# An adaLN block with linear attention and SwiGLU: scale weight in column halves, a fold in three groups, turned weight loads in halves

## The chip, the core and the metric

The kernel runs on one core of a Trainium2 chip. The metric is the device time of one execution in microseconds (us), the median of several runs. TensorE (PE) does matmuls, VectorE (DVE) and ScalarE (ACT) the element work, GpSimd (POOL) small element work and some DMA issues, SyncE (SP) most DMA issues.

## The reference

x is [1, 2048, 1024] in bf16, c is [1, 1024]. Cut to what matters:

```python
mod = (silu(c) @ w_mod).reshape(1, 6, 1, 1024)         # sa, ca, ga, sb, cb, gb
h = layernorm(x) * (1 + ca) + sa
q, k, v = heads(h @ wqkv)                              # 32 heads of 32
pq, pk = phi(q), phi(k)                                # phi(t) = elu(t) + 1 + 1e-6
kv, z = sum_s pk v, sum_s pk
o = (pq kv) / (pq z + 1e-6)
x = x + ga * (o @ wo)
h = layernorm(x) * (1 + cb) + sb
out = x + gb * ((silu(h @ w_gate) * (h @ w_up)) @ w_down)   # inner width 3584
```

## The kernel before, in words

The 2048 tokens are four blocks (sc) of 512, each of four tiles (t) of 128; D = 1024 is eight chunks (cc) of 128. For each block there is a K phase, a V phase and a Q phase of 64 matmuls each (128x128 stationary, 512 moving columns), a kv_phase (lines 335 to 348) that sums phi(K) V per head into kv_acc, and later den (the denominators), wo_tile (lines 631 to 660: attention output times wo, first residual, second layernorm), gate_up (448 matmuls) and down (224). All are issued to TensorE in the order in which the program text calls them: `mm` (line 97) keeps program order. Other engines are ordered by a scheduler, with hand-set anchors (`issue_after`) and, in the start, a fixed order (`in_order`, line 83). Loads are issued on the SP queue in order; where one must follow another, `last_load` (line 117) carries the anchor. Tiles come from pools: k8 (19 buffers of 8 KB per partition, all the big tiles, `big`, line 103) and two PSUM pools of four banks, pa (`acc_a`) and pb (`acc_b`).

**Start (lines 124 to 145 and 465 to 529).** V of block 0 comes first. The first block isn't modulated ahead of V: V uses hs = normalised x times (1 + ca), and the shift sa is added later through vb (line 595). The loads go out in the order x tile 0 and 1, eight chunks of the ca columns of w_mod (wca, tile name wme, 128x1024 each), then wv with x tiles 2 and 3 between, the sa columns (wsa), wk. c is turned on TensorE, passed through Silu (line 479) into scT, and the scale is made by row matvecs with w_mod (`mod_rows`, line 255: four matmuls of 256 columns per chunk into four column groups, and one one-column matmul for the first chunk), turned on DVE (line 263) and multiplied into hs (lines 498 to 504). xn is transposed on TensorE (line 217) and copied by DVE into hT. `keep_warm` matmuls on zeros (lines 456 to 463) fill the waits. sc_row, Silu(c) as a row in all partitions, is made by eight broadcast matmuls and two ACT copies (lines 485 to 489).

**The other blocks.** hT(sc+1) is made in block sc: layernorm (line 242), a transposing DMA per tile on the SP queue (line 239), then eight DVE multiply-adds over 128x512 (`modulate`, line 213, called at line 579). K of block sc+1 needs the result at once (line 543).

**Turned w_mod loads (lines 374 to 398).** The vectors ga, sb and cb are computed on DVE: `mod_load(q)` loads the columns of vector q transposed (two DMAs, each 512 columns, 1 MB, into wmt), and `mod_step` multiplies one 128x1024 piece with sc_row and sums it. The loads of vector 2 (ga) go out at the end of block 0 (line 588), those of 3 (sb) after three K groups of block 1 (line 547), those of 4 (cb) in block 3 (line 558). In block 2 the eight loads of wo go out at that place (lines 550 to 556). `hold_back` (line 369) writes one element of a tile on DVE, so that its load is not issued earlier.

**The fold (lines 602 to 627).** KV is folded into wo: for each half h of the heads, each column half nb and each g, four matmuls (i = 0 to 3) of 32x32 with 512 columns, stationary KVT rows of group g (row group g of the array) and output columns i (column group i). One call does (h, nb) with g = 0 to 3: 16 matmuls, all at different positions of the array, into four PSUM tiles "wf", copied back over wo. The calls stand between Q groups of blocks 1 and 2 (lines 618 to 627).

The lines that the prediction names: L98 is every matmul (helper `mm`), L101 every transpose on TensorE, L121 x loads, L214 modulate, L239 the transposing DMA of hT, L380 the turned load, L498 the first scale, L556 the wo loads.

Of the kernel before, what the change touches and what calls it, by code (L numbers as in the profile page):

```python
# [21 lines left out]
def kernel(  # L22
# [13 lines left out]
    nc = tc.nc  # L36
# [77 lines left out]
    c_sb = const.tile([DC, P], BF16, name="c_sb")  # L114

# [8 lines left out]
    for st in range(2):  # L124
        load_x(st, nc.sync)
# [3 lines left out]
    wca = [big("wme", [4, D]) for _ in range(2)]  # L129
# [6 lines left out]
    for j in range(DC):  # L136
        load_block(wca, wm_v, j, D, nc.scalar if j == 0 else nc.sync)
    for cc in range(DC):
        load_block(wv, wqkv_v, cc, 2 * D)
        if cc in (1, 4):  # L140
            load_x(2 + cc // 4, nc.sync)
# [26 lines left out]
    sc_row = const.tile([P, D], BF16, name="sc_row")  # L168
# [11 lines left out]
    sel = const.tile([P, HPC, P], BF16, name="sel")  # L180
# [17 lines left out]
    def bn(src, mv_out):  # L198
        stats = small.tile([P, NNB, nc.vector.BN_STATS_DIM], F32, name="stats")
        for i in range(NNB):  # L200
            nc.vector.bn_stats(out=stats[:, i, :], in_=src[:, i * NB:(i + 1) * NB])  # L201
        nc.vector.bn_aggr(out=mv_out, in_=stats[:])

    def normalise(dst, src, mean, rstd):
        nc.vector.tensor_scalar(out=dst, in0=src, scalar1=mean, scalar2=rstd, op0=ALU.subtract, op1=ALU.mult)

    def normalise_act(dst, src, mv, rstd):
        nmr = small.tile([P, 1], F32, name="nmr")
        last_nmr[0] = nc.gpsimd.tensor_scalar(out=nmr[:], in0=mv[:, 0, 0:1], scalar1=rstd[:, 0:1], scalar2=-1.0,  # L209
                                op0=ALU.mult, op1=ALU.mult)  # L210
        nc.scalar.activation(out=dst, in_=src, func=ACT.Identity, bias=nmr[:], scale=rstd[:, 0:1])  # L211
# [5 lines left out]
    def pe_transpose_tile(hT, xn, t):  # L217
        tp = acc_b("tp", (DC, P), BF16)
        for cc in range(DC):
            transpose(tp[:, cc, :], xn[:, cc * P:(cc + 1) * P])  # L220
        nc.vector.tensor_copy(out=hT[:, :, t * P:(t + 1) * P], in_=tp[:])
# [3 lines left out]
    def ln1_stats(sc, t):  # L225
        x_sb = x_tiles.pop(sc * STC + t)
        mv = small.tile([P, STC, 2], F32, name="mv")
        bn(x_sb, mv[:, 0, :])
        rstd = rstd_of(mv, 1)
        return sc, t, x_sb, mv, rstd  # L230

    def ln1_norm(sc, t, x_sb, mv, rstd, dve=False):
        xn = k2.tile([P, D], BF16, name="xn", bufs=4)
        if dve:
            normalise(xn[:], x_sb[:], mv[:, 0, 0:1], rstd[:, 0:1])
        else:
            normalise_act(xn[:], x_sb[:], mv, rstd)
        if sc > 0:
            last_load[0] = nc.sync.dma_start_transpose(hTs[sc][:, :, t * P:(t + 1) * P], xn[:])  # L239
        return xn  # L240
# [14 lines left out]
    def mod_rows(q, lo, hi, first=None):  # L255
        for j in range(lo, hi):
            if first is not None:
                mm(first, lhsT=wca[j // 4][:, j % 4, 0:P], rhs=scT[:, j:j + 1], start=False, stop=j == DC - 1)
            row_matvec(mod_ps[:, q * MW:(q + 1) * MW], sc32[:, j, :], (wsa, wca)[q][j // 4][:, j % 4, :],
                       q == 0 and j == 0, j == DC - 1)  # L260
# [4 lines left out]
    def scale_to(hs, hT, cc, lo, hi):  # L265
        nc.vector.tensor_scalar(out=hs[:, cc, lo:hi], in0=hT[:, cc, lo:hi], scalar1=ca0T[:, cc:cc + 1], scalar2=None,
                                op0=ALU.mult)

# [105 lines left out]
    def mod_load(q, cols, held=False):  # L374
        ts = [big("wmt", [DC // 2, D]) for _ in range(2)]
        if held:
            hold_back(ts)
        for h, t in enumerate(ts):
            lo = q * D + h * NB
            last = nc.sync.dma_start_transpose(t[:], w_mod[:, lo:lo + NB])  # L380
            mod_steps.extend((t[:, i, :], cols[:, 4 * h + i:4 * h + i + 1]) for i in range(DC // 2))
        return last
# [71 lines left out]
    nc.vector.memset(sel[:], 0.0)  # L454

    def keep_warm(acc, n):
        for _ in range(n):
            mm(acc[:], lhsT=sel[:, 0, :], rhs=sel[:], start=True, stop=True)

    def keep_warm_f32(acc, n):  # L460
        zeros = sel[:].rearrange("p h n -> p (h n)").bitcast(F32)
        for _ in range(n):
            mm(acc[:, 0:zeros.shape[1]], lhsT=zeros[:, 0:P], rhs=zeros, start=True, stop=True)

    accs = [acc_a() for _ in range(4)]
    spare = accs[3]
    keep_warm_f32(spare, 3)
    keep_warm(spare, 1)
# [5 lines left out]
    with in_order(nc.vector, nc.scalar, nc.gpsimd):  # L474
        mod_ps = acc_b("mod_ps")
        mm(mod_ps[:, 0:DC], lhsT=c_sb[:], rhs=ident[0:DC, 0:DC], start=True, stop=True)
        for g in range(4):
            mm(mod_ps[g * DH:(g + 1) * DH, MW:2 * MW], lhsT=ident[:, 0:DH], rhs=base_t[:, 0:MW], start=True, stop=False)
        nc.scalar.activation(out=scT[:], in_=mod_ps[:, 0:DC], func=ACT.Silu)
        xn0 = ln1_norm(*ln1_stats(0, 0))  # L480
        st1 = ln1_stats(0, 1)
        nc.vector.tensor_copy(out=sc32[:], in_=scT[:].unsqueeze(2).to_broadcast([P, DC, DH]))
        xn1 = ln1_norm(*st1, dve=True)
        keep_warm_f32(spare, 1)
        for h in range(2):
            for j in range(DC // 2):
                mm(accs[h][:, j * P:(j + 1) * P], lhsT=scT[:, 4 * h + j:4 * h + j + 1].to_broadcast([P, P]), rhs=ident[:],
                   start=True, stop=True)
            nc.scalar.copy(out=sc_row[:, h * NB:(h + 1) * NB], in_=accs[h][:])
        keep_warm(spare, 3)  # L490
        first = accs[2][:, 0:1]
        mm(first, lhsT=ident[:], rhs=base_t[:, 0:1], start=True, stop=False)
        mod_rows(1, 0, 3, first)
        pe_transpose_tile(hT, xn0, 0)
        pe_transpose_tile(hT, xn1, 1)
        mod_rows(1, 3, DC, first)
        keep_warm(spare, 1)
        nc.vector.tensor_scalar(out=hs[:, 0, 0:H], in0=hT[:, 0, 0:H], scalar1=first, scalar2=None, op0=ALU.mult)  # L498
        mod_turn(DC, 2 * DC)
        for cc in range(1, 4):  # L500
            scale_to(hs, hT, cc, 0, H)
        xn2 = ln1_norm(*ln1_stats(0, 2))
        for cc in range(4, DC):
            scale_to(hs, hT, cc, 0, H)
        st3 = ln1_stats(0, 3)
        gs = k_groups[0:4]
        v_mms(hs, gs, accs, 0, 6)
        pe_transpose_tile(hT, xn2, 2)
        for cc in range(DC):
            scale_to(hs, hT, cc, H, H + P)  # L510
        xn3 = ln1_norm(*st3)
        v_mms(hs, gs, accs, 6, DC)
        gs2, accs2 = k_groups[4:6], [acc_b("acc") for _ in range(2)]
        v_mms(hs, gs2[0:1], accs2[0:1])
        v_evac(0, gs, accs)
        pe_transpose_tile(hT, xn3, 3)
        for cc in range(DC):
            scale_to(hs, hT, cc, H + P, SCW)
        v_mms(hs, gs2[1:2], accs2[1:2])
        mod_rows(0, 0, DC)  # L520
        mod_turn(0, DC)
        nc.vector.tensor_copy(out=sca[:], in_=scr[:, :, :, 0])
        v_evac(0, gs2, accs2)
        for g in k_groups[6:8]:
            acc = acc_a()
            v_mms(hs, [g], [acc])
            v_evac(0, [g], [acc])
        modulate_all(hT, ca1T, saT)
# [4 lines left out]
    for h in range(2):  # L533
        with tc.issue_after(last_load[0].ins):
            nc.sync.dma_start(out=wq[h][:], in_=wqkv_v[:, 4 * h:4 * h + 4, 0:D])
# [5 lines left out]
    for sc in range(NSC):  # L541
        if sc > 0:
            k_phase(sc, 0, 2)
            kv_phase(sc - 1)
            k_phase(sc, 2, 3)
            if sc == 1:
                mod_load(3, sbT, True)
                mod_step(1)
            k_phase(sc, 3, 4)
            if sc == 2:  # L550
                wo = [big("wo", [4, D]) for _ in range(2)]
                hold_back(wo)
                for h in range(2):
                    for g in range(4):
                        with tc.issue_after(last_load[0].ins):
                            last_load[0] = nc.sync.dma_start(out=wo[h][g * DH:(g + 1) * DH, :, :], in_=wo_v[h, g])  # L556
            if sc == 3:
                mod_load(4, cbT, True)
            k_phase(sc, 4, 8)
        if sc == 0:  # L560
            k_phase(0, 0, 8)
# [24 lines left out]
        if sc == 0:  # L586
            with tc.issue_after(last_load[0].ins):
                last_load[0] = mod_load(2, gaT)

    q_phase(1, 0, 1, 2)  # L590
    q_phase(1, 1, 2)
# [10 lines left out]
    def fold_wo(h, nb):  # L602
        ns = slice(nb * NB, (nb + 1) * NB)
        ps = [acc_b("wf") for _ in range(4)]
        for i in range(HPC):
            for g in range(4):
                rs = slice(g * DH, (g + 1) * DH)
                mm(ps[g][i * DH:(i + 1) * DH, :], lhsT=KVT[rs, h, i * DH:(i + 1) * DH], rhs=wo[h][rs, i, ns],
                   start=True, stop=True)
        for g in range(4):  # L610
            (nc.scalar.copy if g % 2 == 0 else nc.vector.tensor_copy)(out=wo[h][:, g, ns], in_=ps[g][:])

    q_phase(1, 2, 5)
# [5 lines left out]
    den_sum(0, acc_a())  # L619
    fold_wo(0, 0)  # L620
    den_spread(0)
    q_phase(1, 6, 8)
    fold_wo(0, 1)
    q_phase(2, 0, 2)
    fold_wo(1, 0)
    q_phase(2, 2, 4)
    fold_wo(1, 1)
# [3 lines left out]
    def wo_tile(st):  # L631
# [10 lines left out]
        for nb in range(NNB):  # L642
            ns = slice(nb * NB, (nb + 1) * NB)
            a_ps = acc_b("a_ps")
            for hg in range(HG):
                mm(a_ps[:], lhsT=pq[:, hg, t * P:(t + 1) * P], rhs=wo[hg // 4][:, hg % 4, ns],
# [145 lines left out]
```

## Time and profile before

| what | value |
|---|---|
| median of 9 runs | 829.86 us (829.49 to 830.24) |
| profiled execution | 829.49 us, of which span 827.7 us |
| PE busy | 823.3 us, 4609 matmuls |
| DVE, ACT, POOL busy | 348.8, 168.1, 63.9 us |
| first V matmul, first K matmul of block 0 | 10.98, 26.86 us |
| K of block 1, 2, 3 starts | 54.49, 83.37, 112.26 us |
| the four fold groups start | 154.40, 158.32, 162.25, 166.17 us |

The span is the time between the first and the last instruction of the profiled execution; 1.8 us of its own time lie around it. In the timelines each row is a run of like instructions: start in us, length in us, engine, line, operation, output and inputs by the program's names, shape, count, and in brackets the idle time ahead of it and what ended it. The granted clock of TensorE is 1.00 in every window.

### The profile page before, as it was taken

Reading aid. Unit: us, or ns where it says so; the run is one execution under the profiler, and the core shown is the slowest. Engines: PE = TensorE matmul, PEld = TensorE weight load, DVE = VectorE, ACT = ScalarE, POOL = GpSimd, SP = SyncE. Lnnn points to the kernel's source line nnn. Section 1 sums busy time; section 2 is a strip of 40 time slices with the busy share of each in tenths; the row PEclk is TensorE's granted clock in tenths of the full one; section 3 lists DMA queues with packets and bytes.
Section 4 is the critical chain, followed back from the end, with each engine's and each line's share of the span. In section 5 each row is a group of like instructions: output and inputs, shape, how many; then the busy total and the mean of one; then the engine's idle time right before and its main releaser. Section 6 shows DMA issues by size and latency. Waiting matters only on the chain.

```text
span 827.7 us, 11287 instructions
## 1 busy us (share of the span) xinstructions
PE 823.3 (99%) x4609; PEld 379.5 (46%) x4609; DVE 348.8 (42%) x680; ACT 168.1 (20%) x253; POOL 63.9 (8%) x165
## 2 busy tenths in 40 slices
PE   9999999999999999999999999999999999999998
PEld 5444444444444444444444444444444444444444
DVE  6879778886353344421111353211114432222222
ACT  3545443434111101101111010111111101111000
POOL 2101020120312001000000010000001100000000
PEclk9999999999999999999999999999999999999999
DMA  9978444239996836456252272753405529610011
GB/s 351 297 167 195 117 111 102 45 104 324 367 226 201 256 106 184 147 172 206 88 164 90 65 224 88 254 184 109 146 0 183 149 68 358 217 44 1 19 58 51
DMA packets 142212, 129.07 MB, mean 156 GB/s; under 512 B 58768, under 2 KB 120720, under 8 KB 141648
## 3 DMA queue, kind: packets, MB, share of 16 engines
q1 hardware_dynamic: 138208, 115.10, 46.2%
q0 software_dynamic: 3792, 12.98, 5.2%
q8 instruction: 36, 0.59, 0.3%
q10 hardware_dynamic: 160, 0.26, 0.1%
q14 instruction: 16, 0.13, 0.1%
HBM read 101.98 MB, written 12.72 MB: 139 GB/s over the span
## 4 chain that ended last, share of the span: by engine, by line
PE 99%; DVE 0%; issue 0%
PE acc L98 91%; PE a_ps L98 7%; PE kvp L98 1%; PE mod_ps L98 0%; PE tp L101 0%; PE wf L98 0%; PE den L98 0%; PE vb L98 0%; DVE e L708 0%; DVE ob L711 0%; DVE sel L454 0%; DVE neg_half L150 0%
## 5 line engine op out<-in xcount | busy, mean ns | idle before, releaser
L98 PE MATMUL acc<-h2T,wgu 128*128 128x512 bf16 x1792 | 387.6, 379 | 0.0
L98 PEld LDWEIGHTS <-wgu 128*128 128x128 bf16 x1792 | 175.2, 98 | 211.3
L687 DVE TENSOR_TENSOR gu<-acc,e 128x512 bf16<-128x512 f32 x112 | 77.5, 692 | 289.9 <-PE acc L98 289.9
L98 PE MATMUL acc<-wd,gu 128*128 128x512 bf16 (+2 forms) x924 | 196.1, 373 | 0.0
L686 ACT ACTIVATE e<-acc 128x512 f32<-128x512 f32 x112 | 66.9, 597 | 374.8 <-PE acc L98 374.8
L98 PEld LDWEIGHTS <-gu 128*128 128x128 bf16 x924 | 89.3, 98 | 104.4
L708 DVE TENSOR_TENSOR e<-acc,gb_bc 128x512 f32<-128x512 f32 (+2 forms) x33 | 22.3, 676 | 131.7 <-PE acc L98 128.8
L98 PEld LDWEIGHTS <-hT 128*128 128x128 bf16 x448 | 43.6, 98 | 52.2
L98 PE MATMUL a_ps<-wo,pq 128*128 128x512 bf16 x256 | 57.4, 379 | 0.0
L98 PE MATMUL acc<-hT,wq 128*128 128x512 bf16 x256 | 56.7, 379 | 0.0
L98 PE MATMUL acc<-wk,hT 128*128 128x512 bf16 x256 | 56.4, 379 | 0.0
L273 ACT ACTIVATE eb<-acc 128x512 bf16<-128x512 f32 x64 | 37.6, 594 | 61.3 <-PE acc L98 59.0
L211 ACT ACTIVATE xn<-x,nmr,rstd 128x1024 bf16<-128x1024 f32 x16 | 19.8, 1240 | 126.2 <-POOL nmr L209 126.2
L98 PE MATMUL acc<-wv,hT 128*128 128x512 bf16 x192 | 41.9, 379 | 0.0
L98 PEld LDWEIGHTS <-pq 128*128 128x128 bf16 x256 | 25.1, 98 | 30.2
L655 POOL DMA_DIRECT2D x_scratch<-x x16 | 9.8, 615 | 373.9 <-DVE x L648 373.8
L98 PEld LDWEIGHTS <-wq 128*128 128x128 bf16 x256 | 24.6, 98 | 29.9 <-issue 1.1
L274 DVE TENSOR_SCALAR eb<-eb 128x512 bf16<-128x512 bf16 x64 | 18.4, 291 | 25.6 <-ACT eb L273 25.4
L648 DVE TENSOR_TENSOR x<-a_ps,x_sb 128x512 f32<-128x512 f32 x32 | 22.1, 691 | 8.6 <-PE a_ps L98 8.6
L195 POOL TENSOR_TENSOR rstd<-veps,neg_half 128x1 f32<-128x1 f32 x32 | 17.9, 559 | 98.4 <-DVE veps L193 86.3
L201 DVE BATCH_NORM_STATS2 stats<-x_sb 128x6 f32<-128x512 bf16 x32 | 21.0, 675 | 4.5 <-DMA x_sb<-in_A_x_dram 4.4
L711 DVE TENSOR_TENSOR ob<-e,x1r 128x512 bf16<-128x512 f32 (+2 forms) x33 | 22.3, 675 | 1.0
(99 smaller groups left out, 322.2 us busy)
## 6 DMA issues: line engine op xcount, KB each, us to landing
wgu<-in_B_w_gate_dram SPq DMA_DIRECT2D x28, 1024.0 KB, 6.9
wgu<-in_B_w_up_dram SPq DMA_DIRECT2D x28, 1024.0 KB, 8.0
x_sb<-in_A_x_dram SPq DMA_DIRECT2D x32, 256.0 KB, 5.3
x_scratch<-x POOLq DMA_DIRECT2D x16, 512.0 KB, 3.1
x1r<-x_scratch SPq DMA_DIRECT2D x31, 256.0 KB, 2.9
wd<-in_B_w_down_dram SPq DMA_DIRECT2D x7, 1024.0 KB, 6.6
rbc<-rden_scratch POOLq DMA_DIRECT2D x16, 256.0 KB, 8.8
out_dram<-ob SPq DMA_DIRECT2D x31, 128.0 KB, 1.7
```

Source lines behind the costliest of these rows:

```text
L98: return tc.keep_in_program_order(nc.tensor.matmul(out, lhsT=lhsT, rhs=rhs, start=start, stop=stop))
L195: nc.gpsimd.tensor_tensor(out=rstd[:, 0:n], in0=veps[:, 0:n], in1=neg_half[:].to_broadcast([P, n]), op=ALU.pow)
L201: nc.vector.bn_stats(out=stats[:, i, :], in_=src[:, i * NB:(i + 1) * NB])
L211: nc.scalar.activation(out=dst, in_=src, func=ACT.Identity, bias=nmr[:], scale=rstd[:, 0:1])
L273: nc.scalar.activation(out=e[:], in_=acc, func=ACT.Exp)
L274: nc.vector.tensor_scalar(out=e[:], in0=e[:], scalar1=1.0, scalar2=PHI_EPS, op0=ALU.min, op1=ALU.add)
L648: nc.vector.tensor_tensor(out=x1[:, ns], in0=a_ps[:], in1=x_t[:, ns], op=ALU.add)
L655: nc.gpsimd.dma_start(out=x1_dram[st * P:(st + 1) * P, :], in_=x1[:])
L686: nc.scalar.activation(out=sg[:], in_=ps[0][:], func=ACT.Silu)
L687: gm = nc.vector.tensor_tensor(out=guT[sc][f // GPT][:, f % GPT, :], in0=ps[1][:], in1=sg[:], op=ALU.mult)
L708: nc.vector.tensor_tensor(out=yt, in0=y_ps, in1=gb_bc[:, ns], op=ALU.mult)
L711: nc.vector.tensor_tensor(out=ob, in0=yt, in1=x1r, op=ALU.add)
```

## The change

1. *Loads of the start.* Three x tiles first. wca is loaded in two halves of 512 columns, each as four DMAs of 128x2x512 (rows of 1 KB); wv chunks 0 to 3 stand between the halves, x tile 3 and wv 4 to 7 behind.
2. *sc_row.* The broadcast matmuls and ACT copies go. c is loaded as a row, Silu is taken of the row on ACT, it is written to DRAM by POOL and loaded back into all partitions on the SP queue behind wq.
3. *First block.* The scale of chunks 0 to 3 is made as columns by 32 one-column matmuls, that of chunks 4 to 7 by 32 row matmuls of 128 columns inside the V stage. V of the first four groups starts with chunk 0 and goes on as pieces come; hs is scaled directly from PSUM, hT is copied by ACT. All zero-matmuls are f32, of 512, 256 or 128 columns. K of block 0 does its first two groups interleaved.
4. *Turned loads.* (vector 2, half 0) at the end of block 0; (2, half 1) and (3, half 0) in block 1; (3, half 1) in block 2 ahead of the wo loads, which are anchored on it; both halves of 4 in block 3, as before. kv_phase moves from behind K group 1 to behind K group 0.
5. *Fold.* The 16 units (h, nb, g) of four matmuls are done in groups of 5, 6 and 5 units instead of 4 x 4, at three places instead of four, into new tiles wof that wo_tile reads. The PSUM tiles come from both pools.

```diff
-    for st in range(2):
+    for st in range(3):
         load_x(st, nc.sync)
...
-    wca = [big("wme", [4, D]) for _ in range(2)]
+    wca = [big("wme", [DC, NB]) for _ in range(2)]
...
+    def load_ca(h, eng0):
+        for k in range(4):
+            js = slice(2 * k, 2 * k + 2)
+            (eng0 if k == 0 else nc.sync).dma_start(out=wca[h][:, js, :], in_=wm_v[:, js, D + h * NB:D + (h + 1) * NB])
+
+    load_ca(0, nc.scalar)
+    nc.scalar.dma_start(out=sc_row[0:1, :], in_=c)
+    for cc in range(4):
         load_block(wv, wqkv_v, cc, 2 * D)
-        if cc in (1, 4):
-            load_x(2 + cc // 4, nc.sync)
+    load_ca(1, nc.sync)
+    load_x(3, nc.sync)
+    for cc in range(4, DC):
+        load_block(wv, wqkv_v, cc, 2 * D)
...
+        def ca_cols(k):
+            for i in range(4):
+                for j in (2 * k, 2 * k + 1):
+                    mm(cols[i], lhsT=wca[0][:, j, i * P:(i + 1) * P], rhs=scT[:, j:j + 1], start=False,
+                       stop=j == DC - 1 and i in (0, 3))
+
+        mm(cols[0], lhsT=ident[:], rhs=base_t[:, 0:1], start=True, stop=False)
+        mm(mod_ps[:, DC:DC + 3], lhsT=ident[:], rhs=base_t[:, 0:3], start=True, stop=False)
+        keep_warm(NB)
+        ca_cols(0)
+        keep_warm(NB, 2 * P)
+        ca_cols(1)
+        turn_half(xn0, 0, 0)
+        ca_cols(2)
+        keep_warm(P)
+        turn_half(xn0, 0, 1)
+        turn_half(xn1, 1, 0)
+        ca_cols(3)
+        keep_warm(P)
...
+        gs = k_groups[0:4]
+        v_mms(hs, gs, accs, 0, 1)
+        turn_half(xn1, 1, 1)
+        nc.scalar.copy(out=hT[:, 4:8, 0:H], in_=tps[1][:])
+        nc.scalar.activation(out=sc_row[0:1, :], in_=sc_row[0:1, :], func=ACT.Silu)
+        v_mms(hs, gs, accs, 1, 3)
+        tp2 = turn_tile(xn2)
+        for cc in range(4):
+            scale_turned(tp2, cc, 2)
+        nc.scalar.copy(out=hT[:, :, H:H + P], in_=tp2[:])
+        v_mms(hs, gs, accs, 3, 4)
+        ca_rows()
...
+    nc.gpsimd.dma_start(out=sc_dram[:], in_=sc_row[0:1, :])
+    with tc.issue_after(wq_load.ins):
+        nc.sync.dma_start(out=sc_row[:], in_=sc_dram[:].to_broadcast([P, D]))
...
         if sc > 0:
-            k_phase(sc, 0, 2)
+            k_phase(sc, 0, 1)
             kv_phase(sc - 1)
-            k_phase(sc, 2, 3)
+            k_phase(sc, 1, 3)
             if sc == 1:
-                mod_load(3, sbT, True)
+                mod_load(2, gaT, (1,), True)
+                mod_load(3, sbT, (0,), True)
                 mod_step(1)
             k_phase(sc, 3, 4)
             if sc == 2:
+                last_load[0] = mod_load(3, sbT, (1,), True)
                 wo = [big("wo", [4, D]) for _ in range(2)]
...
         if sc == 0:
             with tc.issue_after(last_load[0].ins):
-                last_load[0] = mod_load(2, gaT)
+                last_load[0] = mod_load(2, gaT, (0,))
...
+    wof = [big("wof", [4, D]) for _ in range(2)]
+    fold_units = [(h, nb, g) for h in range(2) for nb in range(NNB) for g in range(4)]
+
+    def fold_wo(accs):
+        units = [(fold_units.pop(0), acc) for acc in accs]
         for i in range(HPC):
-            for g in range(4):
+            for (h, nb, g), acc in units:
                 rs = slice(g * DH, (g + 1) * DH)
...
-    den_sum(0, acc_a())
-    fold_wo(0, 0)
+    den_sum(0)
+    fold_wo([acc_b("wf") for _ in range(3)] + [acc_a() for _ in range(2)])
     den_spread(0)
     q_phase(1, 6, 8)
-    fold_wo(0, 1)
-    q_phase(2, 0, 2)
-    fold_wo(1, 0)
-    q_phase(2, 2, 4)
-    fold_wo(1, 1)
+    q_phase(2, 0, 1)
+    fold_wo([acc_b("wf") for _ in range(4)] + [acc_a() for _ in range(2)])
+    q_phase(2, 1, 4)
+    fold_wo([acc_b("wf") for _ in range(4)] + [acc_a()])
```

## The prediction

> **What bounds the kernel now.** I read the page's busy line first, then its chain of waits, then the timeline of each engine around every place that the diff touches.
>
> ```profile
> PE 823.3 (99%) x4609; PEld 379.5 (46%) x4609; DVE 348.8 (42%) x680; ACT 168.1 (20%) x253; POOL 63.9 (8%) x165
> ...
> PE 99%; DVE 0%; issue 0%
> ```
>
> TensorE (PE) is busy 823.3 of 827.7 us, and the chain that ended last is TensorE too. So a transfer or a vector operation costs nothing until TensorE waits for it, and a change pays or costs only by (a) the length of the matmul stream, (b) a wait put into it, (c) the start ahead of it. There are three such places. The first is the start (timeline of TensorE from 0; columns: start us, length us, engine, operation, count):
>
> ```profile
> 7.18 0.17 PE L98 MATMUL acc<-eb,ident 128*128 128x1 bf16 x1
> 7.21 0.16 PE L98 MATMUL acc<-scT,wme 128*128 128x1 bf16 x1
> ...
> 10.98 5.35 PE L98 MATMUL acc<-wv,hs 128*128 128x512 bf16 x24
> ...
> 22.41 1.06 PE L98 MATMUL mod_ps<-wme,sc 128*32 128x256 bf16 x32
> 23.40 3.63 PE L98 MATMUL acc<-wv,hs 128*128 128x512 bf16 x16
> 26.86 5.34 PE L98 MATMUL acc<-wk,hT 128*128 128x512 bf16 x24
> ```
>
> The first V matmul starts at 10.98 and the first K matmul at 26.86. From there the stream has no gap until the end beyond about 0.09 us where the shape of matmuls changes. The second place is the fold of wo (timeline of TensorE from 153):
>
> ```profile
> 153.84 0.63 PE L98 MATMUL acc<-pq,Zden 128*32 128x128 bf16 x32
> 154.40 0.43 PE L98 MATMUL wf<-wo,kvs 32*32 32x512 bf16 x16
> 154.76 3.63 PE L98 MATMUL acc<-hT,wq 128*128 128x512 bf16 x16
> 158.32 0.43 PE L98 MATMUL wf<-wo,kvs 32*32 32x512 bf16 x16
> 158.69 3.63 PE L98 MATMUL acc<-hT,wq 128*128 128x512 bf16 x16
> ```
>
> Sixteen 32x32 matmuls of 512 columns take 0.367 us together (154.40 to 154.76): each has a tile position of its own, they start 3.3 ns apart, and 317 ns after the last start the next full matmul starts. The third place is the load of hT(3), the normalised block 3 (timelines of SyncE, VectorE and TensorE):
>
> ```profile
> 62.86 8.50 SPq L380 DMA_TRANSPOSE wmt<-in_w_mod_dram  x2
> ```
> ```profile
> 93.91 3.65 SPq L556 DMA_DIRECT2D wo<-in_A_wo_dram  x8
> 100.98 7.06 SPq L239 DMA_TRANSPOSE hT<-xn  x4
> ```
> ```profile
> 110.32 2.68 DVE L214 TENSOR_SCALAR hT<-hT,sca 128x512 bf16<-128x512 bf16 x8 [0.17 <-DMA hT<-xn]
> ```
> ```profile
> 112.25 2.97 PE L98 MATMUL acc<-wk,hT 128*128 128x512 bf16 x13
> ```
>
> VectorE waits 0.17 us for hT(3) and modulates it 110.32 to 113.00; K of block 3 starts at 112.25 and needs the first modulated chunk. That is the smallest cover in the kernel: 112.25 - 110.32 - 0.32 for one chunk = 1.6 us. Now the DMA share over the same time (windows; the last three columns are granted clock, DMA share, GB/s):
>
> ```profile
> 64.40:68.40 4.00, 4.00 (x20) 1.84 (x19) 4.00 (x11) 1.19 (x2) 0.47 (x1) 1.00 1.15 259
> ```
> ```profile
> 95.00:104.60 9.60, 9.60 (x46) 4.40 (x45) 9.04 (x26) 5.43 (x8) 2.77 (x7) 1.00 1.06 223
> 104.60:109.40 4.80, 4.80 (x24) 2.16 (x22) 4.16 (x7) 3.79 (x6) 2.72 (x7) 1.00 1.11 204
> ```
>
> The packets of wo (95.0 to 104.6) and of hT(3) (to 109.4) fill the DMA engines: the share is at or above 1 throughout. One turned w_mod load of 1 MB fills them as well, for 3.9 us (64.4 to 68.4).
>
> **The change, part by part.** All sums are against the profiled execution, 829.49 us (827.7 of span and 1.8 around it). The median shown is 829.86, so I add 0.37 at the end.
>
> *Start.* Prefix: zero-matmuls at half rate to about 4.3 (now 1.21 to 4.49), the c turn and Silu to about 4.7 (now 5.24), a 512-wide f32 zero-matmul (two slow 0.85) to 6.45. Then, at the full rate seen after 6.2: four groups of eight one-column matmuls, 28 ns each (7.18 to 7.21), 0.24 with its switch; three f32 quarters of 0.43, 1.28; 12 transposes of 56 ns, 0.67; one 128-wide f32, 0.21. Sum 6.45 + 0.96 + 1.28 + 0.67 + 0.21 = 9.57, and 0.6 from the last column matmul to the first V matmul, as now (10.42 to 10.98): **10.2**, 0.8 earlier. The V stage then grows: 64 matmuls of 215.8 ns, 13.81; 20 transposes instead of 16, 1.12; the second half of the scale rows moves in, 32 of 128 columns like the den rows (0.56) and a switch, 0.65; sa rows 1.08. Sum 16.66 against 15.88, so 0.8 later. **Net 0.0.** Bounds: one-column matmuls at the 56 ns of a transpose would give +0.9; the weight half may land by about 8.2 (x tiles land 0.67 us apart now, 256 KB in 1 KB rows goes at about 0.75), which allows a first V matmul at 9.0, but the normalise of tile 2 (1.24 on ACT, then eight transposes) is next and leaves about -0.6. So -0.6 to +0.8. The eight broadcast matmuls of sc_row (0.75 at 5.95) and their two ACT copies leave; the list above has them no more. hT copies (0.69 on DVE now) go to ACT, hidden behind V matmuls.
>
> *Fold.* 64 matmuls in groups of 20, 24, 20 instead of 4 x 16. In each step of i the fifth unit has the row group of the first and the same columns: a position that still streams 512 columns. In the trace two matmuls on one position never overlap: the den rows reuse a position each 56 ns, their 128 columns. So each i-step waits 0.216 us, four in a group: 0.367 + 4 x 0.216, less 0.04 since no longer all sixteen starts stand in a row, = 1.19. Three groups and two switches of 0.09 (the first follows den): 3.76; now 4 x 0.367 + 3 x 0.093 = 1.75. **+2.0 us.** If the matmuls behind the waiting one overtook it, all reuse would wait once a group, or not at all: one group less, -0.45, to +0.2. Upper end 2.2.
>
> The Trainium skill, "TensorE: Matmul & The Clock Gate", Part 3 ("What overlaps and what doesn't"), states that matmuls start and end strictly in program order. No row here has a matmul that could overtake another; by the page the sum is the +2.0, without it -0.45 to +0.2 would be open. The page's span model (one matmul and about 4 ns per tile) has the trace's 3.3 ns, but only for distinct tiles, so it speaks against putting 20 into 16 positions.
>
> *A turned load ahead of wo at block 2.* (3, half 1) goes on the SP queue before the eight wo loads; the four hT(3) transposes are queued behind those. 3.9 us of full DMA is put ahead: wo's packets end at 108.5, hT(3)'s at 113.3 instead of 109.4, and the landing moves from 110.2 to 114.1 (or 113.5, if 0.6 of the other traffic seen after 109.4, share 0.92, gives way). The SP issue itself takes 4.0 us (62.86 line, half of 8.50), inside the same delay. VectorE then modulates chunk 0 until 114.5 at the latest; K(3) starts 1.9 to 2.3 after 112.25, say 2.15. For its first group it runs at VectorE's 0.323 per chunk instead of 0.216: 7 x 0.107 = 0.75. What waits behind: all later matmuls. **+2.9 us** (2.6 to 3.05). If the cover were still enough, 0.
>
> *The rest, each 0.* At block 1 two turned loads stand ahead of hT(2), as before; at block 3 two, as before; two instead of one leave the tail of block 0, where nothing waited. kv_phase one K group earlier: its v evictions end 1 us before. The sc_row round trip over DRAM puts 0.67 us into the queue behind wq; its first user is a w_mod step tens of us later. The K pair of block 0: the trace shows 215.8 ns per matmul there without a wait, so nothing to gain. Fold into new tiles: two of 19 buffers, taken from none that is due; evictions (5 of about 0.6 on two engines) lie behind 1.7 us Q groups. If the cover of one of these fails, one transfer's 0.7 us is the size.
>
> **Sum:** 829.49 + 0.0 + 2.0 + 2.9 = 834.4; on the median's side **834.8**, +0.6%.
>
> **Rivals.**
> - *A, both costs as worked out*: 834.8; own range 833.7 to 835.9 (start -0.6 to +0.8, the others' ends). For: share 1.06 to 1.11 leaves no room; one position cannot stream twice. **0.58.**
> - *B, the fold's waits do not hold the others up*: only the stall, 829.86 + 2.9 = 832.8. For: sixteen run together now. Against: nothing in the trace starts out of order. **0.18.**
> - *E, the idle slows TensorE*: at the start it runs at half rate until about 6.2 (128-column matmuls start 107 ns apart, then 56), though the granted clock column says 1.00 there; 5.0 us at half rate lost 2.5. If 2.2 us of waiting bring that back, up to 837.3. Against: waits are short and broken up by eight matmuls. **0.10.**
> - *C, the stall is hidden* because packets of the transposes overtake wo's on the rings; fold only: 831.9. Against: hT(3) landed in issue order, behind wo's 105.4. **0.07.**
> - *D, the other side, faster or the same*: the start. One-column matmuls instead of row groups let the first V matmul begin at the landing of the half weight, 9.0, and tile 2 keeps up: -1.2, and -0.45 if the fold runs free: 828.2. It decides only if the fold and the stall together cost under 1.2. For: now the column matmuls run on to 10.42, with the weight's landings. Against: both costs must vanish. **0.07.**
>
> The Trainium skill, "TensorE: Matmul & The Clock Gate", Part 1, lets the clock fall back after an idle window of about 3.4 us; an estimate by it: our wait of 2.2 us would not trigger E, and if it did the price would be 1.7. No stretch of idle TensorE is in this trace to test it.
>
> **Numbers.** The forecast is A's 834.8. The range takes in A, B and C (0.83) and part of E: 831.9 to 836.6. A measurement of this kernel tells 0.2% (1.7 us) from no change: faster is under 828.2, slower over 831.5. D gives 0.04 faster and 0.03 same; the low ends of C and B give 0.05 same. Faster 0.04, same 0.08, slower 0.88.
>
> **What would show it.** Fold: three groups of 20, 24, 20 records, each some 1.2 us long (0.4 refutes). Stall: TensorE idle near 112, put down to VectorE's hT, and VectorE's modulate waiting for the DMA of hT until about 114. Start: first V matmul near 10.2, first K near 26.9. Wrong, if K(3) starts without a wait, or if the wmt packets of block 2 fall into free DMA time.

## The result and the profile after

The changed kernel takes 834.27 us (median of 10 runs, 832.82 to 838.37) against 829.95 (31 runs, 829.49 to 831.0): 1.0057 times, interval 1.0049 to 1.0065. The forecast was 834.8. Its profiled execution took 833.82 us with a span of 832.0; that of before 829.49 with 827.7.

Page of the changed kernel, the busy line and the head of the chain of waits:

```profile
PE 825.5 (99%) x4623; PEld 379.2 (46%) x4623; DVE 346.3 (42%) x685; ACT 173.8 (21%) x261; POOL 65.2 (8%) x167
...
PE 99%; DMA 0%; DVE 0%; issue 0%; ACT 0%; DVEq 0%
```

TensorE still ends last, but the DMA of hT and VectorE's modulate (L224) have come into the chain. The start, timeline of TensorE:

```profile
10.29 1.04 PE L98 MATMUL acc<-wv,hs 128*128 128x512 bf16 x4
...
26.98 5.34 PE L98 MATMUL acc<-wk,hT 128*128 128x512 bf16 x24
```

The first V matmul is at 10.29 (forecast 10.2), the first K matmul at 26.98 (26.9). The first fold group, and the last (timeline of TensorE from 150):

```profile
158.72 0.39 PE L98 MATMUL wf<-wo,kvs 32*32 32x512 bf16 x3
158.73 0.38 PE L98 MATMUL acc<-wo,kvs 32*32 32x512 bf16 x1
158.74 0.39 PE L98 MATMUL wf<-wo,kvs 32*32 32x512 bf16 x3
...
158.78 0.59 PE L98 MATMUL acc<-wo,kvs 32*32 32x512 bf16 x5
159.31 5.35 PE L98 MATMUL acc<-hT,wq 128*128 128x512 bf16 x24
...
170.47 0.44 PE L98 MATMUL wf<-wo,kvs 32*32 32x512 bf16 x16
170.70 0.42 PE L98 MATMUL acc<-wo,kvs 32*32 32x512 bf16 x4
171.05 5.35 PE L98 MATMUL acc<-hT,wq 128*128 128x512 bf16 x24
```

Twenty matmuls take 0.58 us (158.72 to 159.31), not 1.19. The program issues, for each i, three wf, then two acc; the trace shows one acc per step, and the four fifth ones together at the end, 0.23 us after the first start. In the last group all sixteen of distinct positions run first and the four others 0.23 us later. The matmuls behind a waiting one went ahead of it.

The load ahead of wo: timeline of SyncE, then of VectorE, then of TensorE, then windows (the stretch and its length, busy us and count of TensorE's matmuls, its weight loads, VectorE, ScalarE and GpSimd; the last three columns are granted clock, DMA share, GB/s).

```profile
94.34 4.09 SPq L392 DMA_TRANSPOSE wmt<-in_w_mod_dram  x1
98.60 3.76 SPq L607 DMA_DIRECT2D wo<-in_A_wo_dram  x8
102.47 9.80 SPq L247 DMA_TRANSPOSE hT<-xn  x4
```
```profile
114.21 2.67 DVE L224 TENSOR_SCALAR hT<-hT,sca 128x512 bf16<-128x512 bf16 x8 [3.54 <-DMA hT<-xn]
```
```profile
114.69 3.18 PE L98 MATMUL acc<-wk,hT 128*128 128x512 bf16 x8 [1.75 <-DVE hT L224]
117.79 1.79 PE L98 MATMUL kvp<-v,pk 128*32 128x64 bf16 x128
```
```profile
114.50:115.90 1.40, 1.22 (x4) 0.38 (x4) 1.40 (x6) 0.00 (x0) 0.00 (x0) 1.00 1.07 214
115.90:119.30 3.40, 3.40 (x121) 1.92 (x124) 1.72 (x6) 0.60 (x1) 0.00 (x0) 0.50 0.56 178
119.30:121.00 1.70, 1.70 (x39) 0.85 (x28) 1.70 (x4) 0.00 (x0) 0.12 (x1) 0.99 0.00 0
```

VectorE waits 3.54 us for hT(3), TensorE 1.75 us for VectorE, and then, while TensorE is busy again, its clock is 0.50 for 3.4 us. In the profile before, VectorE waited 0.17 us there, TensorE did not wait and its clock stayed 1.00. The delay already stands in SyncE's row: the four issues of hT(3) took 9.80 us instead of 7.06, the longest 5.33 instead of 2.06. Where the time of the two profiled executions differs, by the starts of the stages on TensorE:

| stretch | before | after | more |
|---|---|---|---|
| to the first K matmul | 26.86 | 26.98 | 0.12 |
| K and Q of block 0 | 27.63 | 27.75 | 0.13 |
| K and V of block 1 | 28.88 | 29.15 | 0.27 |
| K of block 2, with kv_phase | 15.07 | 15.07 | 0.00 |
| V of block 2, to the first K of block 3 | 13.81 | 15.73 | 1.91 |
| K of block 3, with kv_phase | 15.07 | 16.96 | 1.89 |
| from there to the fold | 27.07 | 27.08 | 0.00 |
| first fold group to wo_tile | 17.33 | 17.52 | 0.19 |
| the rest of the span | 655.97 | 655.76 | -0.21 |

The sum is 4.3, the difference of the spans. The 1.89 are 0.76 for VectorE's pace (eight chunks at 0.323, the size seen alone in e3 below) and 1.13, the rest, for the clock. What the -0.21 at the end comes from is not known.

### The profile page after: what moved, and what is told of

It reads as the page before. It is cut to its first block, busy times and chain, and to the rows that moved or that the text cites. A ratio compares the mean times of both kernels' runs of the same rounds, so it can differ in the third digit from the quotient of the medians.

```text
span 832.0 us, 11337 instructions
## 1 busy us (share of the span) xinstructions
PE 825.5 (99%) x4623; PEld 379.2 (46%) x4623; DVE 346.3 (42%) x685; ACT 173.8 (21%) x261; POOL 65.2 (8%) x167
## 4 chain that ended last, share of the span: by engine, by line
PE 99%; DMA 0%; DVE 0%; issue 0%; ACT 0%; DVEq 0%
PE acc L98 91%; PE a_ps L98 7%; PE kvp L98 1%; DMA hT<-xn 0%; PE mod_ps L98 0%; PE den L98 0%; PE tp L101 0%; PE wf L98 0%; PE vb L98 0%; DVE gb_bc L466 0%; DVE hT L224 0%; DVE e L763 0%; DVE ob L766 0%; ACT scT L482 0%; PE col L98 0%
## 5 line engine op out<-in xcount | busy, mean ns | idle before, releaser
L98 PE MATMUL a_ps<-wof,pq 128*128 128x512 bf16 x256 | 57.4, 379 | 0.0
L221 ACT ACTIVATE xn<-x_sb,nmr,rstd 128x1024 bf16<-128x1024 bf16 (+1 forms) x17 | 19.6, 1163 | 14.4 <-POOL nmr L216 14.3
```

The lines of the kernel that those rows point to most:

```text
L98: return tc.keep_in_program_order(nc.tensor.matmul(out, lhsT=lhsT, rhs=rhs, start=start, stop=stop))
L221: nc.scalar.activation(out=dst[:, ws], in_=src[:, ws], func=ACT.Identity, bias=nmr[:], scale=rstd[:, 0:1])
```

## The experiments

Each number below is a median; in brackets the ratio's interval to the kernel before, timed on the same chip.

**e1, the turned loads undone.** Is the load ahead of wo the whole loss?

```diff
             if sc == 1:
-                mod_load(2, gaT, (1,), True)
-                mod_load(3, sbT, (0,), True)
+                mod_load(3, sbT, held=True)
...
             if sc == 2:
-                last_load[0] = mod_load(3, sbT, (1,), True)
...
-                last_load[0] = mod_load(2, gaT, (0,))
+                last_load[0] = mod_load(2, gaT)
```

> The changed kernel with the turned w_mod loads where they were before (both halves of vector 2 at the end of block 0, both of vector 3 in block 1, nothing turned ahead of wo); everything else stays changed. Theory 1 (the profile after: wait for hT(3) 1.9 us, VectorE's pace 0.75, half clock behind the wait 1.1; fold only +0.2): K of block 3 starts without a wait and 3.8 us go, to about 830.4, 0.05% above the kernel before. Theory 2 (the split of the prediction: wait 2.9, fold 2.0): 2.9 us go, to about 831.4.

Measured 831.98 (1.0012 to 1.003): only 2.3 us go. Both theories missed. K of block 3 starts without a wait as theory 1 had it, but this execution lost time in two other places: the first K matmul is at 28.65, and there is a wait in block 1 (timeline of TensorE):

```profile
58.22 1.22 PE L98 MATMUL kvp<-v,pk 128*32 128x64 bf16 x128
59.37 1.25 PE L98 MATMUL acc<-wk,hT 128*128 128x512 bf16 x5
61.47 1.89 PE L98 MATMUL acc<-wk,hT 128*128 128x512 bf16 x8 [0.84 <-issue]
```

"issue" means that TensorE waited for nothing that the profile shows. The page has a DMA queue for instructions, 36 packets of 16 KB, which is 64 B for each of the some 9,200 matmuls and weight loads: one packet holds 256 of them, as many as one kv_phase uses up in 1.15 us. In this execution the packet went at 59.12, while the DMA engines were full (the two turned loads of vector 2 landed at 58.3 and 63.8; in the kernel before at 53.3 and 58.0), and TensorE went on 1.5 us after its end. That the wait is this fetch was not tried apart, but the traces agree on it. In eight of the nine profiles that have the changed start or one close to it (all but e12) TensorE stops for 0.23 to 1.42 us after the same number of its records (matmuls, weight loads and a few semaphores), 961. In e6, whose start has ten records fewer, that is five matmuls later in K. e2 has a second stop 1,024 records on, four times 256. Each time TensorE goes on 1.2 to 1.6 us after the end of an instruction packet.

**e2, the fold in four groups of 16** (into the new tiles).

```diff
-    den_sum(0)
-    fold_wo([acc_b("wf") for _ in range(3)] + [acc_a() for _ in range(2)])
+    den_sum(0, acc_a())
+    fold_wo([acc_b("wf") for _ in range(4)])
...
-    q_phase(2, 0, 1)
-    fold_wo([acc_b("wf") for _ in range(4)] + [acc_a() for _ in range(2)])
-    q_phase(2, 1, 4)
-    fold_wo([acc_b("wf") for _ in range(4)] + [acc_a()])
+    fold_wo([acc_b("wf") for _ in range(4)])
+    q_phase(2, 0, 2)
+    fold_wo([acc_b("wf") for _ in range(4)])
+    q_phase(2, 2, 4)
+    fold_wo([acc_b("wf") for _ in range(4)])
```

> The changed kernel with its fold in four groups of 16 at the old places, still into the new tiles. Theory 1 (matmuls overtake one that waits for its position, so reuse costs one 0.216 per group, and one switch fewer is paid): 0.2 us less, not to be told from the changed kernel in the time, each group 0.367 us in the trace. Theory 2 (strict order, four waits a group): 2.0 us less, 832.3.

Measured 834.24 (1.004 to 1.0065), the same as the changed kernel; each group is 0.367 us again. The fold's regrouping is worth 0.2 us in the trace and nothing that the time shows. Theory 2 falls. In the profiled execution TensorE waited no less ahead of K of block 3, and the clock stayed 1.00: the drop doesn't come every time (more on that at e9). Timeline of TensorE:

```profile
114.74 2.65 PE L98 MATMUL acc<-wk,hT 128*128 128x512 bf16 x8 [2.05 <-DVE hT L224]
```

**e5, two matmuls on one position directly behind each other**, on top of e1, in four groups of 16 as in e2. Settles whether program order binds.

```diff
-    fold_units = [(h, nb, g) for h in range(2) for nb in range(NNB) for g in range(4)]
+    fold_units = [(h, nb, g) for h in range(2) for gp in range(2) for g in (2 * gp, 2 * gp + 1) for nb in range(NNB)]
```

> The kernel of e1 (turned loads undone) with the fold in four groups of 16 whose order puts two matmuls on one array position directly behind each other (g0 nb0, g0 nb1, g1 nb0, g1 nb1, for each i): eight positions, each used twice. Theory 1 (a matmul behind a waiting one starts ahead of it when its own position is free): the first users of all eight positions start within 0.05 us, the second ones 0.2 us later, and each group is about 0.58 us long. Theory 2 (strict program order): each second user holds up all behind it, the starts are in program order with steps of 0.216 us, and a group takes about 1.9 us. The time is not the measure here, the group's length is.

Timeline of TensorE:

```profile
157.21 0.65 PE L98 MATMUL wf<-wo,kvs 32*32 32x512 bf16 x16
157.79 3.63 PE L98 MATMUL acc<-hT,wq 128*128 128x512 bf16 x16
```

A group is 0.58 us (157.21 to 157.79). The sixteen starts fall into two bunches of eight, 157.209 to 157.256 and 157.435 to 157.482, although every second matmul of the program had to wait. Strict order would have made 1.9. Theory 1 holds.

**e3, the wait filled.** Eight zero-matmuls between V of block 2 and K of block 3 in the changed kernel.

```diff
         if sc > 0:
+            if sc == 3:
+                filler = acc_a()
+                for _ in range(8):
+                    mm(filler[:], lhsT=gb_bc[:, 0:P], rhs=gb_bc[:, 0:NB], start=True, stop=True)
             k_phase(sc, 0, 1)
```

> The changed kernel with eight zero-matmuls of 512 columns (1.73 us) between V of block 2 and K of block 3, where TensorE now waits 1.75 us. The arithmetic of the block is untouched. Theory 1 (the wait itself lets the clock drop to 0.50 some us later): the wait for hT(3) stays as long, but the clock stays 1.00 in the 5 us after it, and about 1.1 us go, to 833.1; the spread of the runs (832.8 to 838.4) shrinks too. Rival (the slow stretch after the wait has another cause, such as late evictions or weights): nothing goes, or 1.7 us come if the fill delays K.

Measured 833.56 (1.0034 to 1.0061), 0.7 less than the changed kernel, with runs from 833.32 to 835.59; the two intervals overlap. In its profile the clock is 1.00 throughout, the first K group takes 2.58 us (1.82 without the wait, so VectorE's pace is 0.76) and kv_phase 1.154. The wait did not stay as expected: hT(3) came later, and 1.36 us of idle were left behind the fill. And e2 kept its clock without a fill in its profile, and the start differs from run to run, so this run alone doesn't settle it; e9 repeats it on the steadier kernel.

**e4, the load ahead of wo alone**, in the kernel before.

```diff
-                mod_load(3, sbT, True)
+                mod_load(3, sbT, (0,), True)
...
             if sc == 2:
+                last_load[0] = mod_load(3, sbT, (1,), True)
                 wo = [big("wo", [4, D]) for _ in range(2)]
```

> The kernel before with one thing of the change: half 1 of vector 3 is loaded in block 2 ahead of the wo loads, instead of in block 1. Theory 1: the same wait of 1.7 to 2.2 us ahead of K of block 3, VectorE's pace and the slow clock behind it: +3.8 us, 833.8. Theory 2: +2.9 us, 832.8. Rival (the load is hidden, and the wait of the changed kernel comes from its other edits, such as kv_phase one group earlier or the later start): 829.9.

Measured 834.64 (1.0041 to 1.0067), runs 834.15 to 834.8: +4.7, more than the whole change. The load is not hidden, and alone it suffices. Timeline of TensorE, then windows:

```profile
115.39 5.74 PE L98 MATMUL acc<-wk,hT 128*128 128x512 bf16 x16 [2.32 <-DVE hT L214]
```
```profile
116.80:120.00 3.20, 3.20 (x8) 1.07 (x8) 1.55 (x5) 0.60 (x1) 0.00 (x0) 0.50 0.42 154
```

The wait is longer than in the changed kernel (V of block 2 to K of block 3: 2.49 us more than before), and the clock costs 1.36: two K groups take 5.67 us, 3.55 plus 0.76 without the clock. 2.49 + 0.76 + 1.36 make 4.6 of the 4.7.

**e9, e4 with ten zero-matmuls in the wait.**

```diff
         if sc > 0:
+            if sc == 3:
+                filler = acc_a()
+                for _ in range(10):
+                    mm(filler[:], lhsT=sel[:, 0, :], rhs=sel[:], start=True, stop=True)
             k_phase(sc, 0, 2)
```

> The kernel of e4 (the kernel before, with half 1 of vector 3 loaded ahead of wo in block 2; 834.64, its wait 2.2 us, its clock 0.50 from 116.9 to 120) with ten zero-matmuls of 512 columns (2.16 us) between V of block 2 and K of block 3. Its start is that of the kernel before, whose runs lie close together. Theory (idle TensorE loses its clock some us later, and that is 1.4 us of the 4.7): the wait for hT(3) stays, the granted clock stays 1.00 behind it, and the median falls by 1.4 to about 833.2. Rival (the slow stretch doesn't come from idleness): 834.6 or more.

Measured 833.86 (1.0034 to 1.0059), 0.8 less than e4 and not 1.4. Timeline of TensorE, then windows:

```profile
112.63 2.32 PE L98 MATMUL acc<-sel 128*128 128x512 bf16 x10
115.64 4.38 PE L98 MATMUL acc<-wk,hT 128*128 128x512 bf16 x16 [0.69 <-DVE hT L214]
```
```profile
116.90:120.00 3.10, 3.10 (x21) 1.14 (x24) 1.95 (x6) 0.60 (x1) 0.00 (x0) 1.00 0.50 174
```

The clock is 1.00 where it was 0.50, and the two K groups take 4.31 us instead of 5.67. So idle TensorE does cost its clock. The rest of the expected gain went into hT(3), with which K of block 3 began 0.53 us later behind V of block 2 than in e4, and 0.25 in kv_phase. By the time alone the gain isn't shown, since the two intervals overlap. But the mean granted clock of every run was recorded, and 3.4 us at half clock make it 0.998: it is 0.998 in all five runs of e4, 0.998 in seven of the ten of the changed kernel, 0.997 or 0.998 in three of e2's five, and 0.999 or 1.000 in all ten runs of e3 and e9, which have the fill.

Why e2's profiled wait left the clock alone can be read from the traces. Their record of the granted clock begins at the moment of full rate and changes only at whole multiples of 3.413 us from there: after 32 of them in the changed kernel and 33 in e4, each time for one. In the stretch of 3.413 us that ends with the drop, TensorE was idle 1.75 us in the changed kernel and 2.06 in e4. In e2 such a boundary (113.99) cuts the wait, with 1.29 us on one side and 0.75 on the other; in e3 the stretch holds 1.36 us, and the clock stayed. This was read afterwards; no run moves the boundary.

**e8, both halves of vector 3 ahead of wo**, in the kernel before.

```diff
             if sc == 1:
-                mod_load(3, sbT, True)
...
             if sc == 2:
+                last_load[0] = mod_load(3, sbT, held=True)
                 wo = [big("wo", [4, D]) for _ in range(2)]
```

> The kernel before with both halves of vector 3 loaded in block 2 ahead of wo. Theory 1: 3.9 us more of full DMA than with one half, so hT(3) lands 3.9 us later and TensorE waits about 5.8 instead of 1.9 to 2.3 us; behind it the clock is 0.50 for some 3.4 us, as behind the shorter wait, so about 838.5 (834.6 plus 3.9). Rival (two loads share the engines or the rest of the queue thins out): the second half costs clearly less than 3.9.

Measured 841.57 in one run, +11.7 and not +8.6. The third hT(3) transpose landed at 117.4, 4 us later than with one half, as reckoned; the fourth only at 122.3. GpSimd had issued a broadcast of 256 KB 0.02 us ahead of it; that the two held each other up is read from that, not tried. The wait came to 10.3 us, and the clock was 0.50 for 10.24 us, three times 3.413, most of it while TensorE was idle. Neither theory had that.

**e6, light fill in the start.** e1 with the zero-matmuls behind c in bf16 instead of f32.

```diff
+    def keep_warm_light(*widths):
+        for n in widths:
+            mm(accs[3][:, 0:n], lhsT=gb_bc[:, 0:P], rhs=gb_bc[:, 0:n], start=True, stop=True)
...
-        keep_warm(NB)
+        keep_warm_light(NB)
...
-        keep_warm(NB, 2 * P)
+        keep_warm_light(NB, 2 * P)
...
-        keep_warm(P)
+        keep_warm_light(P)
```

> The kernel of e1 (turned loads undone) with the zero-matmuls of the start that come behind c in bf16 instead of f32: same widths, a quarter of the time. Theory (the changed start is bound by TensorE's own fill until TensorE goes to full rate, and the moment of that differs between executions: 4.8, 6.5 or 10 us in the profiles so far, first V matmul at 9.36, 10.29 or 11.95): the first V matmul comes at 9.0 to 9.8 in each execution, the median goes from 832.0 to about 831.0 and the runs lie closer together. Rival (the start waits for weights or for tile 1, and its spread is that of transfers): nothing changes. Second rival (the light fill leaves TensorE at half rate for longer): the V stage starts at half rate and the time is 832.5 or more.

Measured 832.12 (1.0016 to 1.0038), nothing gained. The first V matmul came at 9.28, as expected, but TensorE did not keep its rate. Timeline of TensorE, then windows:

```profile
8.18 0.61 PE L101 MATMUL tp<-ident,xn 128*128 128x128 bf16 x8
```
```profile
9.40:12.70 3.30, 3.30 (x12) 1.40 (x11) 1.14 (x5) 2.17 (x4) 0.96 (x2) 0.50 1.08 375
```

The eight transposes still run at full rate, 56 ns apart. Then the clock is 0.50: the first four V matmuls take 412 ns each, and the first K matmul was at 27.66. Ahead of that TensorE had waited 1.07 us for columns of w_mod, and it was idle 1.39 us of the 3.413 that end with the drop. The second rival was right that V starts at half rate, though not in the way: full rate had come and was lost again. The time stayed under its 832.5.

**e7, kv_phase back** behind K group 1, on top of e1.

```diff
-            k_phase(sc, 0, 1)
+            k_phase(sc, 0, 2)
             kv_phase(sc - 1)
-            k_phase(sc, 1, 3)
+            k_phase(sc, 2, 3)
```

> The kernel of e1 (turned loads undone) with kv_phase back behind K group 1. Theory (kv_phase uses up 256 instructions of TensorE in 1.15 us, and the fetch of the next 16 KB of them stands behind a turned load; one K group earlier its lead is 1.7 us shorter): the 0.84 us in which TensorE waits for nothing that the profile shows, behind the kv_phase of block 1, goes; the median falls by 0.2 to 1.0 us, to about 831.4. Rival (kv_phase's place is free, as the prediction had it): the same 832.0 and the same wait.

Measured 830.66 (1.0 to 1.0018), 1.3 less than e1. But its profile still has 0.60 us of "issue" inside kv_phase, and its first K matmul was at 26.53 against e1's 28.65, with the same start. So the expectation that this wait goes failed: it comes after 961 records as in e1, and that place now lies inside kv_phase. The two intervals overlap, so whether the edit helps isn't shown: the 1.3 can be the start's draw.

**e11, kv_phase early alone**, in the kernel before.

```diff
-            k_phase(sc, 0, 2)
+            k_phase(sc, 0, 1)
             kv_phase(sc - 1)
-            k_phase(sc, 2, 3)
+            k_phase(sc, 1, 3)
```

> The kernel before with one thing of the change: kv_phase one K group earlier in blocks 1 to 3. Theory (the fetch of TensorE's next 16 KB of instructions has 1.7 us less lead, and in block 1 stands behind a turned load): TensorE waits for nothing that the profile shows 0.3 to 1.0 us behind the kv_phase of block 1, and 0 to 0.5 in blocks 2 and 3: +0.5 to +1.5 us, 830.4 to 831.4. Rival (the place of kv_phase is free): 829.9.

Measured 829.97 (0.999 to 1.0008): no difference, and no such wait. The theory as it stood falls: an earlier kv_phase alone costs nothing here. In e1 the turned loads land some 5 us later than in the kernel before, and its start has 14 matmuls more, so that the packets end at other places of the program; no run parts these two.

**e10, the wait for Silu filled** (e7 with one more zero-matmul at 4.5 us).

```diff
+        keep_warm(P)
         mm(mod_ps[:, DC:DC + 3], lhsT=ident[:], rhs=base_t[:, 0:3], start=True, stop=False)
```

> The kernel of e7 (loads undone, kv_phase back) with one more zero-matmul of 128 columns, f32, between the first and the second base matmul of the start, where TensorE waits 0.2 us for Silu at 4.5 us. Theory (in some executions the idle time around the c turn and Silu keeps TensorE at half rate for one more stretch of 3.4 us, and so comes the spread of the first V matmul, 9.4 to 12.2): full rate comes by 6.7 us in every execution, no run is above 831.2, and the median falls from 830.7 to about 830.2. Rival (the moment of full rate doesn't depend on that gap): the same median and spread (829.4 to 832.2).

Measured 830.11 (0.9994 to 1.0011); three of eleven runs were 831.7 or above. The expectation that no run exceeds 831.2 failed: the gap isn't the cause of the late full rate, or not alone.

**e12, the load behind hT(3)**, and kv_phase back, in the changed kernel.

```diff
-            k_phase(sc, 0, 1)
+            k_phase(sc, 0, 2)
             kv_phase(sc - 1)
-            k_phase(sc, 1, 3)
+            k_phase(sc, 2, 3)
...
-                last_load[0] = mod_load(3, sbT, (1,), True)
...
+        if sc == 2:
+            with tc.issue_after(last_load[0].ins):
+                last_load[0] = mod_load(3, sbT, (1,))
```

> The changed kernel with half 1 of vector 3 loaded behind the four hT(3) transposes of block 2 instead of ahead of wo, and kv_phase back behind K group 1. Theory (only the place of the load in the queue ahead of hT(3) costs, not its being in block 2): K of block 3 starts without a wait, and the time is that of e7, 830.7 within 0.4. Rival (1 MB more of DMA in this block delays hT(3), x or wo wherever it stands, or the w_mod steps of block 3 wait for it and hold up VectorE): 831.5 or more.

Measured 829.99 (0.9993 to 1.0011), the time of the kernel before and 0.7 under e7's, where the same time within 0.4 was expected. Timeline of SyncE, then of TensorE:

```profile
102.87 7.08 SPq L247 DMA_TRANSPOSE hT<-xn  x4
110.04 4.31 SPq L392 DMA_TRANSPOSE wmt<-in_w_mod_dram  x1
```
```profile
114.15 3.62 PE L98 MATMUL acc<-wk,hT 128*128 128x512 bf16 x16
```

K of block 3 starts without a wait, as the theory had it. The same megabyte in the same block costs nothing behind hT(3). The changed start and the new fold are still in this kernel. Eight of its eleven runs lie between 829.5 and 830.1, three between 831.6 and 831.9; the profiled one is of the three. Its start (timeline of TensorE):

```profile
6.92 2.91 PE L98 MATMUL acc<-gb_bc 128*128 128x512 f32 x4
...
11.92 1.04 PE L98 MATMUL acc<-wv,hs 128*128 128x512 bf16 x4
```

From the four f32 records at 6.92 it is 2.7 us to the next matmul at 9.62; in e7's execution the same four went from 6.42 to 7.79. Half rate lasts until 10.5 here, and the first K matmul is at 28.62 instead of 26.53. No version tried is faster than the kernel before beyond its interval.

## Why the prediction was right, and where it wasn't

The time and the sign were right; the sum was right only because two of its errors cancel.

- **Start, 0.0 (-0.6 to +0.8).** In the profiled execution right: first V 10.29, first K +0.12, one-column matmuls 25 to 28 ns. The range was too narrow. The same start gave first K matmuls between 26.06 and 28.86 in the profiles, with TensorE at full rate from 4.7 us in the best and 11.0 in the worst. Before, the prefix had less f32 fill and no such tail (31 runs within 1.5 us). The step took the moment of full rate, 6.2, as given; the boundaries of 3.413 us fall differently in each execution. K and Q of block 0 cost 0.13 more (forecast 0).
- **Fold, +2.0.** Wrong: +0.19. The step that failed is "So each i-step waits 0.216 us, four in a group". The reuse waits once a group, 0.22 us, and one group (0.37) and one mode switch (0.09) are saved. That is rival B's mechanism, given 0.18, and the bound "to +0.2" of the same paragraph. The premise of one wait per reuse was right, the premise that it holds up what is behind it was not (e5, e2).
- **Load ahead of wo, +2.9.** Right: hT(3) landed at 114.09 (forecast 114.1), K of block 3 started at 114.69 (114.4), VectorE's pace cost 0.76 (0.75); 1.91 + 0.76 = 2.67. e4 and e12 show that the place of this load is the cause.
- **The clock, rival E, given 0.10.** It happened: 1.13 us in the profile, 1.36 in e4, recovered in e9. The sum had left it at 0. The argument against it, that the waits are short and broken up, failed: 1.75 us of idle was enough here, though e2's like wait left the clock alone. The prediction's estimate that a wait of 2.2 us would not trigger it failed too; the price it gave for the case, 1.7, is above the measured one.
- **"The rest, each 0".** Block 1 lost 0.27, a wait of TensorE for its instructions by all signs (it went on at 59.07, 1.6 us after the end of an instruction packet); that was on no list.

The terms: 0.25 + 0.19 + 2.67 + 1.13 + 0.27 - 0.21 = 4.3, against the forecast's 0 + 2.0 + 2.9. That this lands near the measured time is luck in part: the fold was 1.8 too dear, and the clock with the smaller terms, at 0 in the sum, made up for most of it. What stays open: why full rate comes late in some executions of the changed start (e10 didn't move it, e6 made it no better), and whether kv_phase's place is worth anything beside the loads.

## What to carry to other kernels

Ask of a moved transfer what is queued behind it and how much cover that has: 1 MB ahead of the one transfer with 1.6 us of cover cost 4.7 us alone, and nothing a few issues later. Price a wait of TensorE with what follows it, the pace of the engine that refills it and the clock after it, which together were as long as the wait itself. And compare a forecast with the trace term by term: a sum that agrees can hide a term that is ten times too large.

## What the runs showed of the hardware

- Matmuls on free 32x32 positions start ahead of an earlier one whose position is busy (e5: two bunches of eight, 0.58 us for sixteen). The Trainium skill, "TensorE: Matmul & The Clock Gate", Part 3, "What overlaps and what doesn't", says that matmuls start in program order without reordering; the measurement decides.
- After 1.75 and 2.3 us of idle the granted clock fell to 0.50, 1.2 and 1.4 us after TensorE had begun again, for 3.413 us (changed kernel, e4); after 1.07 us in the start of e6 and 10.3 us in e8 too. In e2 2.05 us did not do it. The same page, Part 1, has an idle window of about 3.4 us before the clock drops; the length of the slow stretch is that of such a window, but the idle time here was shorter. In these runs, once at full rate, the idle time within one stretch of 3.413 us was 1.39 us or more where the clock then fell and 1.36 or less where it stayed.
- At the start matmuls run at half rate while the granted clock column says 1.00, and the end of that lay at 4.7 to 6.7 us in four and at 10.5 to 11.0 in three of seven executions of one start. In the three, the boundary 3.413 us earlier (7.1 to 7.6) passed without it; with the start before, full rate came at 4.1 to 7.2 in five profiles.
- TensorE waits up to 1.26 us for nothing that the profile shows (e6; 0.84 in e1), with the changed start always after 961 of its records or 1,024 more, and goes on 1.2 to 1.6 us after the end of a 16 KB packet of the instruction queue. That these are waits for instructions is read from that, not tried.
